# A tuned FFT filter and gated MLP kernel: the filter product is summed on GpSimd before one inverse 64-point matmul per frequency, and the set-up is rebuilt

## The chip, the cores and the metric

The kernel runs on one core of a Trainium2 chip. Its time is the time of the whole program on the device in microseconds (us), and lower is better. Every kernel here was run several times. A profile is one such execution: its "span" is a little shorter than the time of the same run.

The engines are PE (matrix multiplication), DVE (VectorE), ACT (ScalarE) and POOL (GpSimd). PEld, in the views, is PE's loading of weights. SP only issues DMAs here. PE writes its results into tiles that the kernel places in PSUM. It keeps eight buffers there: 2 for the hidden layer (`hps`), 3 for the output sums (`acc`) and 3 for the transform (`ps`).

## The reference, cut to what matters

```python
# x: (8, 3008, 256)   filt_r, filt_i: (1505, 256)
X = np.fft.rfft(x, axis=1)
F = (filt_r + 1j * filt_i)[None, :, :]
y = np.fft.irfft(X * F, n=3008, axis=1).astype(np.float32)
# then, with 8 * 3008 = 24064 tokens of width 256, w_in 256 x 2048, w_out 2048 x 256:
h = y.reshape(24064, 256) @ w_in
g = h * (1.0 / (1.0 + np.exp(-beta * h)))
out = (g @ w_out).astype(np.float32)
```

The transform of length 3008 = 47 x 64 is made of four matmul stages: s1 (47 points), s2 (64 points), the filter, s3 (inverse 64 points) and s4 (inverse 47 points). Between s1 and s2, and again between s3 and s4, the data make a round through DRAM (`d`), which reorders them.

## The kernel before

The MLP is cut into 47 blocks of 512 tokens and 16 hidden slices, 752 steps in all. A step is two `hps` matmuls of 512 columns, one activation on ACT, and four `acc` matmuls of 256 columns for the slice of two steps ago. The transform of batch b+1 is interleaved with the MLP of batch b by a plan: unit i of the middle stages does s2 of frequencies 2i and 2i+1, then s3 of the previous unit.

```python
hpsum = ...(tc.tile_pool(name="hpsum", bufs=2, space=PSUM))
opsum = ...(tc.tile_pool(name="opsum", bufs=3, space=PSUM))
fpsum = ...(tc.tile_pool(name="fpsum", bufs=3, space=PSUM))      # s1, s2, s3 and s4 share these three
# ... cut ...
def s2(i):
    def go():
        # ... k0 = 2 * i; (g, kk) = divmod(k0, 6)
        ps = fpsum.tile([P, 2, D], F32, name="ps2", tag="f")
        for e in range(2):
            nc.tensor.matmul(ps[:, e, :], lhsT=t2[...k0 + e...], rhs=st["a2"][g][:, kk + e, :],
                             start=True, stop=True)
        p_t = pqpool.tile([P, 2, D], BF16, name="p_t", tag="p_t")
        q_t = pqpool.tile([P, 2, D], BF16, name="q_t", tag="q_t")
        nc.vector.tensor_tensor(p_t[:], ps[:], fr_sb[:, k0 : k0 + 2, :], ALU.mult)
        nc.vector.tensor_tensor(q_t[:], ps[:], fi_sb[:, k0 : k0 + 2, :], ALU.mult)
def s3(i):
    def go():
        # ... cut ...
        ps = fpsum.tile([P, 2, D], F32, name="ps3", tag="f")
        for e in range(2):
            for tab, src, first in ((t3p, p_t, True), (t3q, q_t, False)):
                nc.tensor.matmul(ps[:, e, :], lhsT=tab[...k0 + e...], rhs=src[:, e, :],
                                 start=first, stop=not first)
        evac(st["z"][:, kk : kk + 2, :], ps[:], both)        # on DVE in batches 1 to 7
# ... cut ...
units = {0: fft_units(0, x_cur, True)}     # batch 0's transform stands ahead of the MLP,
xs[1] = load_x(1)                          # with the loads of filters, weights and tables
```

The layout of the 128 partitions: rows 0 to 63 of s2's `ps` hold the real parts of 64 coefficients and rows 64 to 127 the imaginary parts. The complex product is left to the matmuls: two tables (`t3p`, `t3q`) act on X times the filter's real part and on X times its imaginary part.

## Time and profile before

| | before |
|---|---|
| time, median of 3 runs | 888.96 us (888.82 to 890.35) |
| span of the profiled run | 885.9 us |
| first MLP matmul (`hps`) starts | 110.0 us |
| PE busy | 783.4 us, 88% |
| DVE busy | 414.1 us, 47% |
| POOL busy | 38.2 us, 4% |

First the page of the kernel before: total busy time of each engine, then the busy share in 40 equal slices of 22 us (a digit is tenths; PEclk is the clock granted to PE in tenths of full speed).

```profile
PE 783.4 (88%) x5860; PEld 551.3 (62%) x5953; DVE 414.1 (47%) x691; ACT 543.2 (61%) x789; POOL 38.2 (4%) x79
PE   0023599999999999999999999999999999999997
DVE  6844556545463438335563437435463438331101
PEclk9999799999999999999999999999999999999999
```

Two parts can be read off the PE row. In the first five slices PE is mostly idle: this is the set-up with batch 0's transform, up to 110 us, where the first MLP matmul stands on the timeline (columns: start us, length us, engine, line, operation, operands, number of instructions; a bracket gives the engine's idle time just before and what ended it).

```profile
110.00 1.01 PE L440 MATMUL hps<-y,win_sb 128*128 128x512 bf16 x2 [0.25 <-DVE y L284]
```

From then on PE is at 9 (90% or more) to the end. The next fence is the table of windows for 200 to 300 us of the same run; the columns are the window, its length, then busy us and number of instructions of PE, PEld, DVE, ACT and POOL, then the clock, the DMA share and GB/s.

```profile
200.00:300.00 100.00, 98.16 (x753) 68.97 (x764) 49.43 (x82) 65.93 (x97) 4.14 (x8) 1.00 0.42 111
```

PE is 98% busy at full clock, DVE 49%. The timeline shows what the inverse matmuls of one unit cost on PE (two of the four lines left out).

```profile
541.05 0.27 PE L349 MATMUL ps_6128<-p_t,t3p 128*128 128x256 bf16 x1
...
541.38 0.27 PE L349 MATMUL ps_6128<-q_t,t3q 128*128 128x256 bf16 x1
541.48 0.60 PE L474 MATMUL acc<-wout_sb,gT 128*128 128x256 bf16 x4
```

An instruction's length (0.27 us) is not its cost, because matmuls overlap: from the first start to the start of what follows the four are 0.43 us, and over the whole trace a matmul of 256 columns is followed by the next after 0.109 us (the median). A matmul of 512 columns is followed by the next after 0.216 us.

Last, the view of what PE waited for (tile and line that waited, what ended the wait, total us, times, longest). The longest wait after 110 us is this one:

```profile
PE ps_5985 L324 <- DMA a_5878<-d_5606: 2.0, 1, 2.0
```

It is s2 of one batch standing on the reload of the reordered data.

### The profile page before, as it was taken

What the parts mean: (1) busy time and instruction counts of PE and PEld (TensorE: products, weight loads), DVE (VectorE), ACT (ScalarE), POOL (GpSimd) and SP (SyncE); (2) the same over time, 40 slices, a digit from 0 to 9 for tenths busy, and PEclk for the clock granted to TensorE, in tenths of its full rate; (3) what the DMA queues carried; (4) which work ended last, traced back from release to release, by engine and by line L of the source; (5) the groups of instructions that cost most, each with busy time, mean ns of one, the idle gap of its engine ahead of it and who ended that gap; (6) DMA issues with size and microseconds to landing.
All of it is one profiled execution on the core that took longest, in us unless ns stands there. A gap on an engine that the chain in (4) does not pass through costs nothing.

```text
span 885.9 us, 14752 instructions
## 1 busy us (share of the span) xinstructions
PE 783.4 (88%) x5860; PEld 551.3 (62%) x5953; DVE 414.1 (47%) x691; ACT 543.2 (61%) x789; POOL 38.2 (4%) x79
## 2 busy tenths in 40 slices
PE   0023599999999999999999999999999999999997
PEld 0001466676676767677676767777676767777665
DVE  6844556545463438335563437435463438331101
ACT  1311365666667665776667665676667665777775
POOL 5010010001000000001000000000000000000000
PEclk9999799999999999999999999999999999999999
DMA  9967465517523382507524371504523152501011
GB/s 212 221 146 182 125 120 159 137 37 155 148 85 112 64 197 62 154 26 156 147 79 119 63 198 61 155 26 112 155 79 106 56 150 62 153 26 48 25 48 48
DMA packets 94869, 97.70 MB, mean 110 GB/s; under 512 B 6544, under 2 KB 84880, under 8 KB 94800
## 3 DMA queue, kind: packets, MB, share of 16 engines
q1 hardware_dynamic: 90432, 83.38, 31.5%
q0 software_dynamic: 4368, 13.37, 10.4%
q8 instruction: 46, 0.75, 0.3%
q14 instruction: 23, 0.19, 0.1%
HBM read 60.30 MB, written 49.81 MB: 124 GB/s over the span
## 4 chain that ended last, share of the span: by engine, by line
PE 77%; DMA 14%; DVE 4%; issue 2%; ACT 1%; SPq 1%; DVEq 0%; ACTq 0%
PE acc L474 34%; PE hps L440 31%; DMA fr_sb<-in_filt_r_dram 5%; DVE ost L486 2%; DMA ws<-in_moe_w_out_dram 1%; DMA d_676<-a_738 1%; DMA d_1769<-a_1985 1%; DMA d_3048<-a_3264 1%; DMA d_5606<-a_5822 1%; DVE q_t L334 1%; DMA d_319<-a_347 1%; DMA zz<-d_677 1%; DMA d_676<-a_838 1%; DMA d_319<-a_375 1%; SPq L259 1%
## 5 line engine op out<-in xcount | busy, mean ns | idle before, releaser
L449 ACT ACTIVATE gT<-hps,beta_sb 128x512 bf16<-128x512 f32 x752 | 515.8, 687 | 252.6 <-PE hps L440 217.4
L474 PE MATMUL acc<-wout_sb,gT 128*128 128x256 bf16 x3008 | 456.7, 273 | 5.1 <-DVE ost L486 0.9
L440 PE MATMUL hps<-y,win_sb 128*128 128x512 bf16 (+7 forms) x1635 | 429.6, 351 | 0.5 <-DVE y L284 0.3
L474 PEld LDWEIGHTS <-gT 128*128 128x128 bf16 x3008 | 287.2, 98 | 143.3 <-issue 6.8
L440 PEld LDWEIGHTS <-win_sb 128*128 128x128 bf16 x1728 | 165.0, 98 | 25.6 <-issue 1.7
L486 DVE COPY ost<-acc 128x512 f32<-128x512 f32 x94 | 60.2, 681 | 123.1 <-PE acc L474 123.0
L386 PEld LDWEIGHTS <-zz 96*128 96x128 bf16 x512 | 36.5, 102 | 35.5 <-DMA zz<-d_320 7.7
L303 PEld LDWEIGHTS <-t_129 94*96 94x96 bf16 x128 | 16.7, 132 | 58.3 <-issue 53.1
L324 PEld LDWEIGHTS <-t_131 128*128 128x128 bf16 x192 | 19.2, 100 | 40.6 <-issue 20.9
L80 POOL DMA_DIRECT2D xg<-in_x_dram x32 | 17.2, 536 | 570.2 <-PE ps_6948 L303 85.1
L303 PE MATMUL ps_343<-xg,t_129 94*96 94x512 bf16 x1 | 0.6, 586 | 31.2 <-ACT a_333 L280 31.2
L349 PEld LDWEIGHTS <-t3q 128*128 128x128 bf16 x192 | 19.1, 99 | 8.7 <-issue 5.6
L349 PEld LDWEIGHTS <-t3p 128*128 128x128 bf16 x192 | 19.1, 99 | 5.7 <-DVE p_t L333 0.8
L81 POOL DMA_DIRECT2D xg<-in_x_dram x32 | 16.4, 513 | 1.6 <-DMA xg<-in_x_dram 1.6
L303 PE MATMUL ps_351<-xg,t_129 94*96 94x512 bf16 x1 | 0.6, 586 | 14.8 <-DVE a_333 L282 14.8
L137 DVE TENSOR_TENSOR r<-u,r 128x1536 f32<-128x1536 f32 x6 | 10.5, 1758 | 0.2
L280 ACT ACTIVATE a_347<-ps_351 96x512 bf16<-96x512 f32 x1 | 0.6, 592 | 16.1 <-PE ps_351 L303 16.1
L165 PE MATMUL tp<-ident,t_129 94*96 94x94 bf16 x1 | 0.3, 312 | 11.3 <-DVE t_129 L161 11.3
L138 ACT ACTIVATE t_131<-r 128x1536 bf16<-128x1536 f32 x2 | 3.0, 1483 | 10.7 <-DVE r L137 10.7
L324 PE MATMUL ps_397<-a_389,t_131 128*128 128x256 bf16 x2 | 0.6, 397 | 9.0 <-DMA a_389<-d_319 9.0
L264 DVE TENSOR_SCALAR wout_sb<-ws,rbeta_sb 128x256 bf16<-128x256 f32 x16 | 4.6, 348 | 7.7 <-DMA ws<-in_moe_w_out_dram 7.7
L138 ACT ACTIVATE t3p<-r 128x1536 bf16<-128x1536 f32 x2 | 3.0, 1483 | 7.5 <-DVE r L137 7.5
(1158 smaller groups left out, 622.3 us busy)
## 6 DMA issues: line engine op xcount, KB each, us to landing
out_dram<-ost SPq DMA_DIRECT2D x47, 512.0 KB, 2.9
xg<-in_x_dram POOLq DMA_DIRECT2D x32, 320.0 KB, 5.3
fr_sb<-in_filt_r_dram SPq DMA_DIRECT2D x16, 192.0 KB, 6.9
fi_sb<-in_filt_i_dram SPq DMA_DIRECT2D x16, 192.0 KB, 8.6
ws<-in_moe_w_out_dram SPq DMA_DIRECT2D x4, 512.0 KB, 5.9
xg<-in_x_dram POOLq DMA_DIRECT2D x32, 56.0 KB, 5.6
d_320<-z SPq DMA_DIRECT2D x4, 384.0 KB, 2.7
zz<-d_320 SPq DMA_DIRECT2D x4, 384.0 KB, 5.5
```

Source lines behind the costliest of these rows:

```text
L80: nc.gpsimd.dma_start(t[:80], xv[:80, js, :])
L81: nc.gpsimd.dma_start(t[80:NP], xv[80:NP, js, :])
L137: nc.vector.tensor_tensor(r, u, r, ALU.subtract)
L259: nc.sync.dma_start(ws[:], moe_w_out[f0 * P : (f0 + WG) * P, :].rearrange("(fb fp) j -> fp fb j", fp=P),)
L303: nc.tensor.matmul(ps[:KP], lhsT=t1[:], rhs=xg[g][:, jj : jj + 2, :], start=True, stop=True)
L324: nc.tensor.matmul(ps[:, e, :], lhsT=t2[:, k0 + e, :, :].rearrange("p c k -> p (c k)"), rhs=st["a2"][g][:, kk + e, :], start=True, stop=True,)
L349: nc.tensor.matmul(ps[:, e, :], lhsT=tab[:, k0 + e, :, :].rearrange("p c k -> p (c k)"), rhs=src[:, e, :], start=first, stop=not first,)
L386: nc.tensor.matmul(ps[:, e, :NP], lhsT=zz[:, j0 % JG + e, dc * P : (dc + 1) * P], rhs=t4[:], start=True, stop=True,)
L440: nc.tensor.matmul(hps[:, pos - t0 : pos - t0 + ln], lhsT=win_sb[:, dc, fb * P : (fb + 1) * P], rhs=ys[b][:, dc, n0 : n0 + ln], start=(dc ...
L449: nc.scalar.activation(gT[:, :tn], hps[:, :tn], ACT.Silu, scale=beta_sb[:, fb : fb + 1])
L474: nc.tensor.matmul(acc[tb // 2][:, tb % 2, :], lhsT=gT[:, tb * P : (tb + 1) * P], rhs=wout_sb[:, fb, :], start=(fb == 0 and tb % 2 == 0), ...
L486: nc.vector.tensor_copy(ost[:, 2 * h : 2 * h + n, :], acc[h][:, :n, :])
```

## The change

The intent has three parts.

1. **Filter product summed on GpSimd.** In batches 1 to 7 the complex product is finished before the inverse matmul. DVE makes `a_t` = X fr, and with two instructions on 64 partitions each `b_t`, whose upper half is -(lower half of X) fi and whose lower half is (upper half of X) fi. GpSimd adds them to `yh`. One matmul per frequency with one table is then enough, two per unit in place of four. Batch 0 keeps the two products.
2. **Set-up.** The filters are loaded once and copied to the other 64 partitions on chip. The tables come from integer phases (folding by shifts), and the inverse table from TensorE transposes of the forward one. `wout`'s scaling moves from DVE to GpSimd.
3. **Plan.** s1 of the next batch runs a batch ahead. s2 and s3 stand two units apart instead of one, over a longer stretch. The units keep out of steps 15, 0 and 1 of each block of 16, where DVE empties the output sums.

```diff
     def s2(b, i):
-        p_t = pqpool.tile([P, 2, D], BF16, name="p_t", tag="p_t")
-        q_t = pqpool.tile([P, 2, D], BF16, name="q_t", tag="q_t")
-        nc.vector.tensor_tensor(p_t[:], ps[:], fr_sb[:, k0 : k0 + 2, :], ALU.mult)
-        nc.vector.tensor_tensor(q_t[:], ps[:], fi_sb[:, k0 : k0 + 2, :], ALU.mult)
+        ps, ks = s2_matmuls(b, i)
+        nc.vector.tensor_tensor(a_t[:], ps[:], fr_sb[:, ks, :], ALU.mult)
+        nc.vector.scalar_tensor_tensor(b_t[:M], ps[M:], -1.0, fi_sb[:M, ks, :], ALU.mult, ALU.mult)
+        nc.vector.tensor_tensor(b_t[M:], ps[:M], fi_sb[:M, ks, :], ALU.mult)
+        nc.gpsimd.tensor_tensor(yh[:], a_t[:], b_t[:], ALU.add)
     def s3(b, i):
         for e in range(2):
-            for tab, src, first in ((t3p, p_t, True), (t3q, q_t, False)):
-                nc.tensor.matmul(ps[:, e, :], lhsT=tab[...], rhs=src[:, e, :], start=first, stop=not first)
+            nc.tensor.matmul(ps[:, e, :], lhsT=t3[:, k0 + e, :], rhs=yh[:, e, :], start=True, stop=True)
# ... cut: loads, tables ...
-                nc.vector.tensor_scalar_mul(wout_sb[:, f0 + i, :], ws[:, i, :], rbeta_sb[...])
+            nc.gpsimd.tensor_tensor(wout_sb[:, f0 : f0 + WG, :], ws[:], rbeta_sb[...].broadcast_to([P, WG, D]), ALU.mult)
# ... cut ...
+    QUIET = (15, 0, 1)
+    def clear(s):
+        s = int(round(s))
+        while s % NFB in QUIET:
+            s += 1
+        return s
+        a, z = (0.30, 0.70) if first else (0.06, 0.64)
+        for i, s in enumerate(spread(f(a), f(z), NU + 2)):
+            s = clear(s)
+            if i < NU:
+                at(s, s2, b, i)
+            if i >= 2:
+                at(s, s3, b, i - 2)
+    for g in range(4):          # after the wout products in program order
+        load_x(1, g)
```

## The prediction

> What bounds the kernel now. The page gives a span of 885.9 us, in two parts.
>
> Set-up with batch 0's transform: the timeline shows the first expert matmul (hps) only at 110 us; PE is nearly idle for 80 us while DVE and DMA are busy. The chain of waits explains it: filter loads until 41 us, the w_out loads (ws) to 59 us, then wout's scaling on DVE; the first stage's evictions (a) stand behind that in DVE's order and resume at 60 us, although data and PE were ready at 11 us.
>
> Main part, 110 to 886 us: bound by PE. The windows show PE 97 to 99% busy at clock 1.00, ACT 66%, DVE 50%. On the timeline a 256-column matmul follows the previous one after 0.109 us, a 512-column one after 0.216 us[...]. So only fewer columns or fewer stalls help. Summed over all matmuls after 112 us, issue at that rate is about 751 us; the remaining 18 us are a throttled start (clock 0.83 in 110-120) and waits for the reloaded a tiles at each batch's start (PE 8.0, 9.0, 9.2, 8.0 us busy in the 10 us windows at 130, 220, 320, 520).
>
> What changes on PE. In batches 1 to 7 the inverse product takes 2 matmuls per unit instead of 4: 168 fewer of 256 columns at 0.109 us, minus 18.4 us, all on the critical path. First-stage work is planned a batch ahead, so most waits for a should vanish: minus 7 us.
>
> What moves. DVE pays three multiplications per unit (about 0.69 us each by p_t's duration: 2.1 instead of 1.3 us), GpSimd one addition[...]. A unit comes every 4 us with two units of slack: off the path. DVE should reach 55 to 60% in the main part.
>
> Set-up. Half the filter bytes (16 loads of 192 KB fewer, landing every 0.85 us in the trace), smaller tables, no DVE wait for ws. First-stage evictions should run at 15 to 25 us; then ACT's copies (10 of 1.0 to 1.5 us) and the reload of a let the 12 frequency units (1.28 us each, as before) run from about 37 to 55 us; first hps at 68 us, 42 us sooner.
>
> Part is given back: GpSimd's order puts batch 1's x loads after the four wout products, which need ws, queued behind the zz loads. I put the products' end at 78 us ([...]two load rounds of 4 to 6 us) and x landing (5.3 us) at 84 to 86 us. PE meets batch 1's first stage at step 1, so it should idle from about 70 to 85 us. Before, that matmul ran at 111.5 us: net set-up gain 26 us.
>
> Sum: 889 - 26 - 18.4 - 7 = about 838 us.
>
> Right if: 168 inverse matmuls fewer; first hps near 68 us; a PE gap of 10 to 18 us soon after, released by xg; PE about 99% afterwards; GpSimd adds never releasing a late PE. Wrong if: first hps later than 80 us (ACT copies or a's reload slower); the gap absent (about 825) or over 20 us; evictions on the longer DVE queue stall PE at block ends; GpSimd and DVE slow each other.
>
> Chances: faster by over 2% 0.96, within 2% 0.03, slower 0.01. Range 822 to 855 us.

The sum came to 889 - 26 - 18.4 - 7 = about 838 us. The products' end at 78 us, and so the gap's end and the 26 us, contain four of the product times. That the addition is off the path rested in part on its time; after the change it took 1.27 us and a product 1.89 us.

## The result, and the profile after

| | before | after |
|---|---|---|
| time, median | 888.89 us (888.40 to 890.35) | 857.02 us (855.05 to 861.43) |
| ratio | | 0.9648 (95% interval 0.9615 to 0.9681) |
| span of the profiled run | 885.9 us | 859.7 us |
| first `hps` matmul | 110.0 us | 73.1 us |
| PE busy | 783.4 us | 776.8 us |
| DVE / POOL busy | 414.1 / 38.2 us | 453.1 / 158.1 us |

The before column is from the runs made beside the changed kernel. A ratio here is the mean time of one kernel's runs over the mean of the other's of the same rounds, so it is not quite the ratio of the medians quoted beside it. The profiled run of the changed kernel was its slowest, 861.43 us.

The kernel became 3.5% faster, but it is 19 us slower than predicted and 2 us outside the range. The page after, as before:

```profile
PE 776.8 (90%) x5809; PEld 538.7 (63%) x5809; DVE 453.1 (53%) x722; ACT 554.2 (64%) x805; POOL 158.1 (18%) x169
PE   2253888989999999999999999999999999999997
DVE  6272259746656476556656476466656467240101
PEclk9995799999999999999999999999999999999999
```

PE starts real work one or two slices sooner, then is at 8 for several slices where before it was at 9. The first `hps` matmul, and the gap that follows soon after:

```profile
73.14 1.86 PE L474 MATMUL hps<-y,win_sb 128*128 128x512 bf16 x4 [0.16 <-DVE y L120]
87.09 1.06 PE L133 MATMUL ps<-xg,t 94*96 94x512 bf16 x2 [12.09 <-DMA xg<-in_x_dram]
```

The same window as before, and the waits of PE:

```profile
200.00:300.00 100.00, 97.98 (x763) 69.06 (x761) 60.43 (x94) 67.50 (x100) 20.43 (x21) 1.00 0.41 111
```

```profile
PE ps L400 <- DVE b_t L391: 15.1, 16, 2.2
PE ps L133 <- DMA xg<-in_x_dram: 12.7, 2, 12.1
```

The predicted 99% in the main part did not come: PE is 98% busy, as before. The waits for the reloaded `a` there are gone, as predicted; the 9.0 us of waiting for it that the full list has is one wait in the set-up. The gap before batch 1's first stage came too (12.1 us, released by `xg`). What was not expected is the first line: the inverse matmul (L400) waited 16 times, 15.1 us in all, for `b_t`, the last filter product on DVE. These two do not even belong together: L400 reads `yh`, not `b_t`. The groups behind it (busy us, mean ns of one, then idle time of the engine just before them):

```profile
L392 POOL TENSOR_TENSOR yh<-a_t,b_t 128x512 bf16<-128x512 f32 x84 | 106.5, 1267 | 404.9 <-DVE b_t L391 404.9
L387 DVE TENSOR_TENSOR a_t<-ps,fr_sb 128x512 f32<-128x512 f32 x84 | 57.7, 687 | 78.9 <-PE ps L155 78.8
L388 DVE SCALAR_TENSOR_TENSOR b_t<-ps,fi_sb 64x512 f32<-64x512 f32 x84 | 58.2, 693 | 1.1
L391 DVE TENSOR_TENSOR b_t<-ps,fi_sb 64x512 f32<-64x512 f32 x84 | 57.4, 683 | 1.1
L400 PE MATMUL ps<-yh,t 128*128 128x256 bf16 x168 | 32.1, 272 | 15.1 <-DVE b_t L391 15.1
```

DVE's costs were estimated well (three times 0.69 us), and GpSimd's addition takes 1.27 us. So the error lies in how they meet. One of the 16 waits on the timeline, all engines, with lines left out:

```profile
219.47 1.29 DVE L505 COPY ost<-acc 128x512 f32<-128x512 f32 x2 [2.76 <-PE acc L494]
...
219.92 0.38 PE L155 MATMUL ps<-a,t 128*128 128x256 bf16 x2
...
220.14 0.38 PE L400 MATMUL ps<-yh,t 128*128 128x256 bf16 x2
...
220.68 0.68 DVE L387 TENSOR_TENSOR a_t<-ps,fr_sb 128x512 f32<-128x512 f32 x1
...
221.23 0.38 PE L155 MATMUL ps<-a,t 128*128 128x256 bf16 x2
221.37 0.69 DVE L388 SCALAR_TENSOR_TENSOR b_t<-ps,fi_sb 64x512 f32<-64x512 f32 x1
...
222.08 0.68 DVE L391 TENSOR_TENSOR b_t<-ps,fi_sb 64x512 f32<-64x512 f32 x1
222.79 0.69 DVE L118 CAST z<-ps 128x512 bf16<-128x512 f32 x1
...
222.91 0.27 PE L400 MATMUL ps<-yh,t 128*128 128x256 bf16 x1 [1.30 <-DVE b_t L391]
222.93 1.27 POOL L392 TENSOR_TENSOR yh<-a_t,b_t 128x512 bf16<-128x512 f32 x1 [5.51 <-DVE b_t L391]
```

Count the three transform buffers. s2 of unit i (219.92) takes the first, s3 of unit i-2 (220.14) the second, s2 of unit i+1, only one step later (221.23), the third. The s3 behind it needs the first again. DVE began to read that one only at 220.68, after the block-end copy `ost`, and held it through three products until 222.76. PE idles 1.30 us and goes on at 222.91. GpSimd had been idle for 5.5 us.

Units come one step apart because the plan pushes units out of steps 15, 0 and 1 of a block: their distances in batches 2 to 7 are 4, 4, 4, 5, 4, **7, 1**, 5, 4, 6, **2**, 5, 4 steps, and in batch 1, which is squeezed into less time, they go down to 0.

A second thing costs time in batch 1. Windows of the changed kernel, same columns:

```profile
98.40:101.80 3.40, 1.28 (x9) 0.66 (x8) 1.20 (x2) 1.23 (x3) 0.00 (x0) 1.00 0.75 192
101.80:105.20 3.40, 3.40 (x14) 1.85 (x13) 0.78 (x2) 2.17 (x4) 0.00 (x0) 0.50 0.44 131
125.70:129.10 3.40, 1.23 (x10) 0.79 (x9) 3.34 (x6) 0.96 (x2) 0.20 (x1) 1.00 0.43 144
129.10:132.50 3.40, 3.40 (x14) 1.81 (x12) 3.02 (x5) 0.69 (x1) 1.95 (x2) 0.50 0.03 11
```

Three of the four waits of over 2 us in batch 1 are followed by 3.4 us at half clock (at 101.8, 129.1 and 176.9 us), which costs some 1.7 us more each time. One of the three was a wait for `b_t`; the other two were waits for an eviction `a` on DVE that in turn waited for the store of an earlier `a` (2.1 and 2.2 us). The fourth, for `b_t` and just as long as the other one for it, was not followed by it:

```profile
150.51 0.38 PE L400 MATMUL ps<-yh,t 128*128 128x256 bf16 x2 [2.17 <-DVE b_t L391]
```

So the length of a wait alone does not decide; what does was not shown. The waits of 1.3 us in later batches were not followed by half clock either: the window of 200 to 300 us, which has such waits, ran at 1.00.

### The profile page after: what moved, and what is told of

It reads as the page before. It is cut to its first block, busy times and chain, and to the rows that moved or that the text cites. A ratio compares the mean times of both kernels' runs of the same rounds, so it can differ in the third digit from the quotient of the medians.

```text
span 859.7 us, 14835 instructions
## 1 busy us (share of the span) xinstructions
PE 776.8 (90%) x5809; PEld 538.7 (63%) x5809; DVE 453.1 (53%) x722; ACT 554.2 (64%) x805; POOL 158.1 (18%) x169
## 4 chain that ended last, share of the span: by engine, by line
PE 80%; DVE 6%; DMA 4%; issue 2%; POOL 1%; ACT 0%; SPq 0%; DVEq 0%; ACTq 0%; POOLq 0%
PE acc L494 36%; PE hps L474 35%; PE ps L133 3%; DMA d<-a 2%; PE ps L188 2%; PE ps L400 2%; DVE ost L505 2%; PE ps L155 1%; DVE b_t L391 1%; DVE a_t L387 1%; DVE b_t L388 1%; DMA zz<-d 1%; POOL wout_sb L368 1%; DMA xg<-in_x_dram 0%; DMA ws<-in_moe_w_out_dram 0%
## 5 line engine op out<-in xcount | busy, mean ns | idle before, releaser
L392 POOL TENSOR_TENSOR yh<-a_t,b_t 128x512 bf16<-128x512 f32 x84 | 106.5, 1267 | 404.9 <-DVE b_t L391 404.9
L118 DVE CAST a<-ps 96x512 bf16<-96x512 f32 x112 | 76.0, 682 | 75.8 <-PE ps L133 52.2
L120 DVE TENSOR_SCALAR y<-ps 128x376 bf16<-128x376 f32 x120 | 65.4, 548 | 75.6 <-PE ps L188 73.5
L387 DVE TENSOR_TENSOR a_t<-ps,fr_sb 128x512 f32<-128x512 f32 x84 | 57.7, 687 | 78.9 <-PE ps L155 78.8
L133 PE MATMUL ps<-xg,t 94*96 94x512 bf16 x128 | 51.5, 422 | 27.8 <-DMA xg<-in_x_dram 12.7
L118 DVE CAST z<-ps 128x512 bf16<-128x512 f32 x84 | 58.1, 692 | 30.5 <-PE ps L400 28.3
L388 DVE SCALAR_TENSOR_TENSOR b_t<-ps,fi_sb 64x512 f32<-64x512 f32 x84 | 58.2, 693 | 1.1
L391 DVE TENSOR_TENSOR b_t<-ps,fi_sb 64x512 f32<-64x512 f32 x84 | 57.4, 683 | 1.1
L188 PE MATMUL ps<-t,zz 96*128 96x94 bf16 x512 | 43.5, 215 | 10.0 <-DMA zz<-d 7.5
L155 PE MATMUL ps<-a,t 128*128 128x256 bf16 x192 | 37.4, 279 | 9.4 <-DMA a<-d 9.0
L400 PE MATMUL ps<-yh,t 128*128 128x256 bf16 x168 | 32.1, 272 | 15.1 <-DVE b_t L391 15.1
L400 PEld LDWEIGHTS <-t 128*128 128x128 bf16 x168 | 15.4, 97 | 23.6 <-issue 14.2
```

The lines of the kernel that those rows point to most:

```text
L118: nc.vector.tensor_copy(dst, src)
L120: nc.vector.tensor_scalar_mul(dst, src, scale)
L133: nc.tensor.matmul(ps[:KP], lhsT=t1[:], rhs=xg[b, g][:, jj : jj + 2, :], start=True, stop=True)
L188: nc.tensor.matmul(ps[:, e, :NP], lhsT=zz[:, j0 % JG + e, dc * P : (dc + 1) * P], rhs=t4[:], start=True, stop=True,)
L387: nc.vector.tensor_tensor(a_t[:], ps[:], fr_sb[:, ks, :], ALU.mult)
L388: nc.vector.scalar_tensor_tensor(b_t[:M], ps[M:], -1.0, fi_sb[:M, ks, :], ALU.mult, ALU.mult)
```

## The experiments

Three theories of the waits on `b_t`: Theory A: a transform buffer in PSUM is held by the three products, because s2 stands ahead of s3 and the quiet steps bunch units. Theory B: GpSimd's sum comes late. Theory C: DVE simply has too much work, so that a wait removed in one place comes back in another. In the expectations, 17.7 us is the same sum of 16 waits as the 15.1 us above, counted from start to start of the matmuls beyond the distance without a wait (0.109 us after 256 columns) instead of as idle time, which makes each wait 0.16 us longer.

All twelve kernels gave results that agree with the reference. They ran on four chips; each of the first three shared its runs of the kernel before, whose medians there were 889.79 us (e1 to e4), 887.95 (e5 to e8) and 888.49 (e9 to e11); beside e12 it was 889.52. All edits are to the changed kernel.

### e1_no_quiet: no quiet steps

```diff
-    QUIET = (15, 0, 1)
+    QUIET = ()
```

> Edit: units are no longer moved out of steps 15, 0 and 1 of a block, so none share a step. Theory A (PSUM): in the changed kernel the inverse product waits 17.7 us in all, each wait ended by DVE's last product b_t, because units pushed together make it reuse a PSUM buffer that the unit just issued still holds for three DVE products (2.1 us). Then the waits of batches 2 to 7 (2.05 us each) fall below 0.3 us per batch, the two of 2.3 us in batch 1 vanish with their slow clock, and the time is 840 to 847 us; waits for ost grow by at most 3 us. Rival C (DVE simply has too much work): the waits only move to ost and the time stays within 3 us of 857. Rival B (GpSimd's sum comes too late) would also be helped here, so this run does not tell A from B.

Measured: 860.96 us (858.43 to 861.53), ratio 0.9689 (0.9645 to 0.9733). No gain at all. PE's waits:

```profile
PE acc L494 <- DVE ost L505: 16.1, 19, 2.5
...
PE ps L400 <- DVE b_t L391: 1.5, 6, 0.4
```

The bunching does cause the waits on `b_t`: they fell from 15.1 to 1.5 us. But an equal amount came up where the quiet steps had kept it away. The accumulator of the next block waits for `ost`, whose copy now stands behind three products (1.4 us in the changed kernel, 16.1 here). So with s2 ahead of s3 the quiet steps are needed, and the expected gain of theory A was a miss: this edit moves the collision and does not remove it. That the waits move to `ost` is what theory C had forecast, so by itself e1 speaks for C; e2, which leaves DVE's work as it is, decides against it.

### e2_s3_first: s3 ahead of s2 within a unit

```diff
         for i, s in enumerate(...):
-            if i < NU:
-                at(s, s2, b, i)
             if i >= 2:
                 at(s, s3, b, i - 2)
+            if i < NU:
+                at(s, s2, b, i)
```

> Edit: within a unit the older inverse product is issued before the new forward product; nothing else. A: where two units share a step, the second inverse product now takes the third, free buffer; the new wait is that the second forward product needs the first inverse product's eviction (0.7 us, perhaps after ost). Waits on b_t fall from 17.7 to under 5 us, time 843 to 850. B (GpSimd's sum late): the inverse product is asked for earlier, so its waits stay at 17 us or grow, time 857 or more.

Measured: 845.05 us (844.74 to 845.52), ratio 0.9516 (0.9475 to 0.9557). That is 12 us better than the changed kernel, for two swapped statements. The timeline at the same place, the same pair of units one step apart:

```profile
214.88 1.29 DVE L505 COPY ost<-acc 128x512 f32<-128x512 f32 x2 [2.96 <-PE acc L494]
...
215.33 0.38 PE L400 MATMUL ps<-yh,t 128*128 128x256 bf16 x2
...
215.55 0.38 PE L155 MATMUL ps<-a,t 128*128 128x256 bf16 x2
...
216.09 0.68 DVE L118 CAST z<-ps 128x512 bf16<-128x512 f32 x1
...
216.63 0.38 PE L400 MATMUL ps<-yh,t 128*128 128x256 bf16 x2
216.69 0.68 DVE L387 TENSOR_TENSOR a_t<-ps,fr_sb 128x512 f32<-128x512 f32 x1
...
216.85 0.38 PE L155 MATMUL ps<-a,t 128*128 128x256 bf16 x2
```

Now the buffer that comes round again is the one of s3, which DVE frees with a single copy `z` by 216.77 us, in time for the s2 at 216.85. The wait is gone, though the units are as bunched as before. The waits of L400 on `b_t` left the list (one of 0.9 us is left, of s1), and it waits for its real operand instead, much less:

```profile
PE ps L400 <- POOL yh L392: 2.7, 4, 1.3
```

And the window of 200 to 300 us shows the predicted 99%, with DVE as busy as before (62% against 60%), so theory C falls:

```profile
200.00:300.00 100.00, 99.08 (x759) 70.42 (x770) 61.91 (x98) 69.20 (x102) 20.89 (x22) 1.00 0.43 116
```

### e3_sum_on_dve: the sum on DVE

```diff
-        nc.gpsimd.tensor_tensor(yh[:], a_t[:], b_t[:], ALU.add)
+        nc.vector.tensor_tensor(yh[:], a_t[:], b_t[:], ALU.add)
```

> Edit: the addition runs on DVE[...] instead of GpSimd. A: the buffer comes free at the same b_t, so each wait stays as it is or grows by up to 0.7 us where two units are processed in a row; b_t or yh ends 17 to 27 us of waits, time 857 to 868. B: the waits come from GpSimd's 1.27 us, they shrink by about half, time 845 to 850.

Measured: 860.46 us (859.25 to 861.96), ratio 0.9684 (0.9634 to 0.9735). The waits stayed, a little longer:

```profile
PE ps L400 <- DVE b_t L391: 17.6, 18, 2.8
```

With GpSimd out of the chain the waits are as before. Theory B falls.

### e6_four_buffers: a fourth transform buffer

```diff
-    opsum = ...(tc.tile_pool(name="opsum", bufs=3, space=PSUM))
-    fpsum = ...(tc.tile_pool(name="fpsum", bufs=3, space=PSUM))
+    opsum = ...(tc.tile_pool(name="opsum", bufs=2, space=PSUM))
+    fpsum = ...(tc.tile_pool(name="fpsum", bufs=4, space=PSUM))
```

> Edit to the changed kernel: one PSUM buffer is moved from the output accumulators (3 to 2) to the transform (3 to 4); order and work unchanged. A (the inverse product waits for a buffer): the waits ended by b_t fall from 17.7 us to under 4 us; in exchange the accumulators wait for ost at each of 47 block starts, about 0.7 to 1.5 us each, so the time is 850 to 895 and says nothing alone. B (the sum is late): the b_t waits stay near 17 us.

Measured: 861.44 us (859.80 to 861.71), ratio 0.9710 (0.9676 to 0.9743).

```profile
PE acc L494 <- DVE ost L505: 8.5, 32, 0.5
...
PE ps L400 <- POOL yh L392: 2.4, 4, 1.0
```

This is theory A tested directly. With one buffer more, and nothing else of the order changed, L400 waits no more for `b_t` and only 2.4 us for its real operand. The time does not show it, because the fourth buffer was taken from the accumulators: with two instead of three, the start of a block waits for `ost` (0.5 us at most, 32 times). Counted from start to start, like the 17.7 us of `b_t`, these waits come to 14.3 us.

### e4_two_matmuls: the filter product undone

The rest of the change is kept.

```diff
-        nc.vector.tensor_tensor(a_t[:], ps[:], fr_sb[:, ks, :], ALU.mult)
-        nc.vector.scalar_tensor_tensor(b_t[:M], ps[M:], -1.0, fi_sb[:M, ks, :], ALU.mult, ALU.mult)
-        nc.vector.tensor_tensor(b_t[M:], ps[:M], fi_sb[:M, ks, :], ALU.mult)
-        nc.gpsimd.tensor_tensor(yh[:], a_t[:], b_t[:], ALU.add)
+        nc.vector.tensor_tensor(p_t[:], ps[:], fr_sb[:, ks, :], ALU.mult)
+        nc.vector.tensor_tensor(q_t[:], ps[:], fi_sb[:, ks, :], ALU.mult)
# s3: two matmuls, t3 with p_t and t3q with q_t; t3q is kept for all batches
```

> Edit: the filter product alone is undone in batches 1 to 7 (two full products on DVE in bf16, two inverse matmuls per frequency), schedule and set-up stay as changed. PE gets 168 matmuls of 0.109 us back: +18.3 us. A: the buffer is held for two products (1.3 us) instead of three (2.1), so each of the 14 large waits shrinks by 0.7 us and the slow-clock episodes after 2.3 us waits go: waits 17.7 to about 8 us, time 857 + 18 - 10 - 3 = 862 (858 to 868). If the waits vanish wholly the time is 853 to 857; if they are as long as before 875. The prediction's own sum (waits nil in both) would give 857 + 18 = 875.

Measured: 860.62 us (859.28 to 862.01), ratio 0.9691 (0.9648 to 0.9734). The 168 matmuls of 0.109 us that it has more are worth 18.3 us of PE, yet it is only 3.6 us slower (860.62 - 857.02), as theory A expected (858 to 868 us). The two medians come from different chips, and the intervals of the two ratios (0.9691 and 0.9648) overlap, so these 3.6 us are not clear of noise; that they are far from 18.3 is. With two products (688 + 681 ns) the buffer is free sooner than with three (2.06 us), and little waits on it:

```profile
PE ps L394 <- DVE q_t L386: 3.2, 8, 1.1
```

So of the 32 us that the change gained, about 28 came from the set-up and the plan (889 to 860.6), and about 4 from the filter product, which gives 12 of its 18 us back as waits on the third product (15.1 - 3.2). The remaining 3 us of the difference were not traced.

### e10_two_matmuls_ordered: the same, with the waits mended

e4 with the order of e2 and the early loads of e5 (below); its counterpart is e9.

> Edit: as the previous kernel, but the filter product is undone in batches 1 to 7 (two products, two inverse matmuls per frequency). In the changed kernel's order this undoing cost only 3.6 us of the 18.3 us that PE's columns are worth. If the rest was lost to waits for the PSUM buffer, then with the order mended the filter product is worth nearly all of it: this kernel is 13 to 18 us slower than the previous one, 847 to 852 us. If the filter product is worth little for another reason (DVE or GpSimd load), the difference stays under 6 us: 834 to 840.

Measured: 851.21 us (849.34 to 853.08), ratio 0.9581 (0.9554 to 0.9607). Against e9 (836.80 us, same chip) the filter product is worth 14.4 us, as expected, against 3.6 in the order of the change. The columns were always worth it; the order spent it.

### e5_x_first: batch 1's x ahead of the wout products

```diff
+        for g in range(4):
+            load_x(1, g)
         tiny = sp.tile(...)        # wout's scaling follows
# ... and the same loop taken away after s4 of batch 0
```

> Edit to the changed kernel: the loads of batch 1's x are issued on GpSimd ahead of the four wout products (the prediction's 'given back' step). If the 12.5 us PE gap at 87 us is only the x loads standing behind the products, PE's next obstacle is the first activation, which waits for GpSimd to finish wout at about 82 us: the gap shrinks to about 9 us. The x traffic then competes with the first batch's reloads between 27 and 47 us, which may delay the first hps by 0 to 8 us. Time 850 to 860; the wait at the first batch-1 matmul falls from 12.5 to under 1 us and a wait for gT or wout of 5 to 9 us takes its place.

Measured: 845.92 us (845.25 to 849.21), ratio 0.9541 (0.9508 to 0.9575), 11 us better than the changed kernel.

```profile
PE ps L402 <- DVE b_t L393: 15.7, 17, 2.2
...
PE ps L133 <- DMA xg<-in_x_dram: 1.0, 1, 1.0
```

The gap of 12 us is gone, and the waits on `b_t` are what they were: the two faults are independent. First `hps` is later (76.4 us against 73.1). The expectation was too pessimistic: it supposed that another wait would take most of the gap's place. Only some of it was taken: the set-up's wait for the reloaded `a` is 13.2 us against 9.0.

### e9_order_and_x: both edits

e2 and e5 together.

> Edit: the inverse-product-first order (845.1 us alone) and the earlier x loads (845.9 us alone) together, on the changed kernel (857.0). If the waits for a PSUM buffer (17.7 us) and the wait for x (12.5 us) are separate causes, the gains of 12.0 and 11.1 us add: 834 us (831 to 838). If one only shifts to the other: 840 or more.

Measured: 836.80 us (832.36, 835.30, 838.30 and 842.47), ratio 0.9440 (0.9395 to 0.9484). Twelve and eleven us, less 3, and within the expected 831 to 838: the two causes are separate. It has the lowest median of all kernels here and beats both kernels of the change, by 5.6% and by 2.4% (836.80 / 857.02 = 0.976, of medians from different chips).

### e7_one_product: one product for both halves (on e2)

DVE multiplies by `fi` once on all 128 partitions, and GpSimd swaps the halves.

```diff
-        nc.vector.scalar_tensor_tensor(b_t[:M], ps[M:], -1.0, fi_sb[:M, ks, :], ALU.mult, ALU.mult)
-        nc.vector.tensor_tensor(b_t[M:], ps[:M], fi_sb[:M, ks, :], ALU.mult)
+        nc.vector.tensor_tensor(c_t[:], ps[:], fi_sb[:, ks, :], ALU.mult)
+        nc.gpsimd.tensor_copy(b_t[:M], c_t[M:])
+        nc.gpsimd.tensor_copy(b_t[M:], c_t[:M])
# fi_sb's copy is negated for the sign, and t3q's sign moved accordingly
```

> Edit, on top of the inverse-product-first order (845 us): DVE forms the fi product over all 128 partitions in one instruction instead of two of 64 (each of those costs a full 0.69 us), and GpSimd swaps its halves with two copies (0.5 us each, from the 64x1536 copy of 1.46 us) before its addition. DVE saves 0.69 us per unit, 58 us in all; GpSimd goes to about 2.3 us per unit. If DVE's length is what makes batch 1's closely spaced units wait (about 5 us in the 845 us version), the time is 840 to 844; if GpSimd's longer chain matters instead, batch 1 gets slower (waits on yh over 5 us) and the time is 846 to 852.

Measured: 843.61 us (840.69 to 845.35), ratio 0.9504 (0.9470 to 0.9539). Against e2 that is 1.4 us, within the spread of the runs: inconclusive. Waits for `yh` rose from 2.7 to 4.3 us.

### e8_ws_early: w_out loaded and scaled during batch 0's units (on e2)

```diff
+        for n in range(3):
+            load_ws(n * WG)            # before batch 0's units; staging buffers 2 -> 3
         for i in range(NU + 1):
+            if i == 5: scale_wout()    # three products on GpSimd
+            if i == 7: load_ws(3 * WG); scale_ws(3)
```

> Edit, on top of the inverse-product-first order (845 us): w_out is loaded and scaled during batch 0's frequency units instead of after its zz loads, so GpSimd is free for batch 1's x about 20 us sooner. If the gap before the first batch-1 matmul (12.8 us) comes from that queueing, it falls to 0 to 4 us; x and ws traffic may delay zz and the first hps by up to 4 us. Time 832 to 840.

Measured: 841.07 us (835.58 to 841.67), ratio 0.9465 (0.9425 to 0.9505): a half-miss. The gap before batch 1's first stage fell to 0.7 us, but batch 0 now waited longer for its own data, and first `hps` came at 81.1 us instead of 71.9 in e2:

```profile
PE ps L188 <- DMA zz<-d: 16.9, 4, 12.1
```

In e2 PE waited 9.7 us for `zz`, here 16.9 us, with the loads of w_out issued during batch 0's round through DRAM. Moving them earlier trades one wait for most of another.

### e11_setup_too and e12_fi_on_gpsimd: more of the set-up off ACT

e11 is e9 and e7 with the `fi` copies made on GpSimd as multiplications by -1, the loads of w_in and of batch 1's x held back until the first reloaded `a` has landed, and batch 1's stages spread over more steps.

```diff
-            nc.scalar.activation(fi_sb[M:, ks, :], fi_sb[:M, ks, :], ACT.Copy, scale=-1.0)
+            nc.gpsimd.tensor_scalar(fi_sb[M:, ks, :], fi_sb[:M, ks, :], -1.0, None, ALU.mult)
+        nc.gpsimd.tensor_copy(gate[:], st["a2", 0, 0][:, 0, :1])
         nc.gpsimd.dma_start(win_sb[:], ...)
-            s1_at(1, f(0.0) + 1, f(0.17), True)
+            s1_at(1, f(0.0) + 1, f(0.15), True)
-        a, z = (0.30, 0.70) if first else (0.06, 0.64)
+        a, z = (0.26, 0.70) if first else (0.06, 0.64)
```

> Edit: as the first kernel of this call, and further: one fi product over all partitions with GpSimd's swap, the copies of fi on GpSimd instead of ACT (ACT's run from 38.3 to 43.9 us and the first z eviction stood behind them at 44.6 us), win and x of batch 1 issued only once the first reloaded tile of batch 0 has landed, so that the stores of a no longer share the DMA engines with them (8.3 us instead of 3 us to land), and batch 1's units spread over 35 instead of 32 steps. Expected: first z eviction at about 40 us, first hps near 71 us (76 us in the version with early x), batch 1 waits 3 us shorter: 824 to 830 us. If the reload of a stays late, first hps stays at 75 to 76 us and the time is 831 to 834.

Measured: 841.71 us (840.43 to 843.24), ratio 0.9474 (0.9450 to 0.9499): a clear miss, no better than e9. The timeline of e11, where it goes wrong:

```profile
11.73 4.11 POOL L322 TENSOR_SCALAR fi_sb<-fi_sb 64x1536 f32<-64x1536 f32 x1 [0.43 <-DMA fi_sb<-in_filt_i_dram]
...
11.88 4.38 DVE L286 TENSOR_SCALAR u<-vi,ms,off 128x768 int32<-128x768 int32 x1
```

The same DVE instruction of the changed kernel, beside which GpSimd does no multiplication but a plain copy:

```profile
11.81 0.68 DVE L286 TENSOR_SCALAR u<-vi,ms,off 128x768 int32<-128x768 int32 x1
```

GpSimd's multiplication took 4.1 us where its copy of the same size took 1.73, and the DVE instruction beside it took 4.38 us instead of 0.68, ending just after GpSimd's. Three instructions of DVE beside such multiplications took so long (4.38, 4.29 and 3.83 us, against 0.68, 0.68 and 0.18 us in the changed kernel), and the tables, ready by 16 us in the changed kernel, were ready only at 25.6. First `hps` came at 84.7 us. What couples the two engines was not shown. In the main part of the changed kernel nothing like it is seen: the 20 `a_t` and 17 `b_t` products that overlapped an addition on GpSimd took 0.68 and 0.69 us, as the others did.

e12 therefore is e9 with plain `fi` copies on GpSimd and the same spread of batch 1.

```diff
-            nc.scalar.activation(fi_sb[M:, ks, :], fi_sb[:M, ks, :], ACT.Copy)
+            nc.gpsimd.tensor_copy(fi_sb[M:, ks, :], fi_sb[:M, ks, :])     # in a loop after the fr copies
# and the two lines of batch 1 as in e11
```

> Edit: the mended order with early x loads (836.8 us), and: the copies of fi are plain copies on GpSimd, after its four copies of fr (1.46 us each, when DVE's tables are done) instead of on ACT, so win and x are issued 6 us later; batch 1's units spread over 35 steps instead of 32. The version with GpSimd multiplications by -1 (4.1 us each) in between failed because DVE's table instructions of 0.68 us took 4.4 us while one of those ran; here no GpSimd instruction of set-up but the first copy meets the tables. If that was its fault: first hps at 70 to 74 us (76.3 us before the edit), time 828 to 833. If instead win and x now hold up the reload of a: first hps at 76 us or later, time 835 to 840.

Measured over six runs: 840.50 us (836.36 to 843.34), ratio 0.9446 (0.9416 to 0.9475): the other branch of the expectation. The copies left ACT's queue, but PE waited 17.0 us for the reloaded `a` (12.7 us in e9), with w_in and x issued from 31.6 us on; the first `z` came at 52.3 us and first `hps` at 80.6 us. One premise of e11 and e12 does not hold in the changed kernel's trace: there ACT had been idle for 0.70 us before the first `z` (44.62 us) and was released by PE, so ACT's copies were not what held it. The difference of e12 from e9 lies within the spread of e9's own runs, so neither kernel is shown better.

## Why the prediction was wrong

The direction was right (faster by over 2%, given 96%); the time was not: 857 us against 838, with a range up to 855.

**The step that failed** is this one: "A unit comes every 4 us with two units of slack: off the path." The slack was reckoned for `yh`, the operand of the inverse matmul, and there it held: the list of PE's waits after names none for `yh`, GpSimd was idle 5.5 us before the addition shown, and e3 shows that its place does not matter. What was not reckoned is the slack of the PSUM buffer that the products read. Three products hold it for 2.06 us (687 + 693 + 683 ns) instead of two for about 1.4 (692 + 681 ns in the kernel before). A unit takes two of the three buffers, one of them for s2. And units do not come every 4 us: the quiet steps put some one step (1.3 us) or less apart, where the kernel before had them an even 2.4 us apart. The prediction did name "evictions on the longer DVE queue stall PE at block ends" among what could make it wrong, but put no time on it. The cause is shown from three sides: an additional buffer removes the wait (e6), freeing the short-held buffer first removes it (e2, 12 us), and even spacing removes it (e1), though there and in e6 another wait took its place.

Point by point:

- **Set-up, first hps at 68 us**: 73.1 measured, 5 us late. Units were to start about 37 us, but the first reloaded `a` landed only at 41.7 us, because the last two stores of `a` took 8.3 and 7.4 us beside the w_in load (3.0 and 2.8 us for two of the stores in e11, where w_in is issued after them); the first `z` came at 44.6. The mis-sized term is the round of `a` through DRAM.
- **The gap from about 70 to 85 us, released by xg**: right, from 75.0 to 87.1. The reason was right too: with x loaded first it falls from 12.1 to 1.0 us and the kernel gains 11 us (e5). Against the prediction the end of the gap is only 2 us late.
- **168 fewer inverse matmuls, minus 18.4 us, "all on the critical path"**: the count was right (L400 x168), and so was the place on the path. But the change kept about 4 us of it (after against e4, not clear of noise) and 14.4 with the order mended (e9 against e10). The rest went into the failed step.
- **Waits for a, minus 7 us**: right for the reloaded `a`, no wait for it is left after the set-up. In batch 1 two new waits, for evictions of `a`, cost 4.3 us.
- **DVE at 55 to 60%**: 60% in the window from 200 to 300 us. Also right, and no sign of trouble: e2 has 62% in the same window and no such waits. A share of busy time says nothing about how long a buffer is held.
- **Clock**: not in the prediction. Three stretches of half clock in batch 1 cost about 5 us, one of them after a wait for `b_t`.

Added up, the unpredicted costs are 15.1 us (waits on `b_t`), about 5 (clock), 4.3 (waits on `a` in batch 1) and 2 (end of the gap), 26 us. The miss is 19 (23 for the profiled run, 861.43 us, in which these costs were read). It is the smaller number since the prediction had kept 11 us of old stalls, of which an unknown part is used up by these. With the one order mended, e2 still stands 7 us above 838; the late end of the gap and the remaining waits are candidates, and how they share it was not separated.

## What to carry to other kernels

When work is moved from PE to DVE, count how long each PSUM buffer is held, and let the stage whose buffer is freed by one short instruction take its buffer first; that swap was worth 12 us here and cost nothing. Check a "slack of n units" against the smallest distance between units in the plan, not the mean, since a rule that pushes work away from one place can bunch it at another, as the quiet steps did here. When an experiment shows no gain, read which wait replaced the old one before dropping the theory: e1 and e6 each removed 13 to 15 us of waiting on `b_t` and showed no faster time.

## What these traces show of the hardware

- Half clock: in batch 1 of the changed kernel three of four idle times of PE of 2.1 to 2.2 us were followed by 3.4 us at a granted clock of 0.50. In the 3.4 us before the two stretches that are shown, PE was still busy for 1.28 and 1.23 us. The fourth, of 2.17 us, and the waits of 1.3 us were not followed by it, so no threshold comes out of these traces.
- GpSimd: 1.27 us for an addition of 512 elements per partition, 1.89 us for the `wout` product of 1024 elements per partition. A copy of 64x1536 f32 took 1.46 to 1.73 us, but a multiplication by a constant of the same tile 4.1 us (e11).
- A DVE product on 64 partitions took as long as one on 128: 0.693 and 0.683 us for 64x512, against 0.687 us for 128x512.
